# Spectral filter plus token mixer: the array shapes of two TensorE steps in the filter stage

## The chip, the cores and the metric

The kernel runs on one core of a Trainium2 chip. The metric is the device time of one execution in microseconds, and lower is better. Times of the kernel before are the median of three runs, and one execution was taken with the hardware profiler.

## The reference

The input is a matrix of 2048 tokens by 640 channels. Two kinds of layer alternate, and each pair is applied twice:

```python
# A: spectral filter
X = rfft2(layernorm(x), axes=(tokens, channels))   # 2048 x 321 complex
x = x + irfft2(X * (w_r + 1j * w_i))
# B: token mixer
h = layernorm(layernorm(x))
u = gelu(einsum("bsd,sf->bdf", h, w1) + b1)        # over the 2048 tokens, F = 1728
x = x + (einsum("bdf,fs->bds", u, w2) + b2).T
# x = A, B, A, B with the same weights
```

All of it is in float32; the kernel splits operands into a high and a low float16 part and multiplies three products (high by high, high by low, low by high).

## The kernel before

A filter layer is written as matrix products. The transform over the tokens is done in two factors, 2048 = 128 x 16, and the transform over the channels in one. Step by step, with the names of the code:

- `a0` normalizes and folds the rows and multiplies by the first token factor (table `tM`). Its output is `s1h` and `s1l`, the high and the low half of one array.
- `a1` is the **filter stage**. It is the part that is changed, and it runs twice in the program (from 60 to 130 us and from 560 to 628 us of the profiled span). It works through 16 groups, g = 0 to 15, and one group takes these steps:
  - **d** (`dstage`): the transform over the channels. The stationary operand is a piece of `s1h` or `s1l` (or `stk`, a stack of remainders that a DMA puts together), and the table `tD` streams through. The output is a PSUM tile `ps` with two banks, `ps[:, 0]` and `ps[:, 1]`.
  - **ph**, **pl** (`psplit`): ScalarE copies `ps` to float16 (`ph`), VectorE takes the rest (`pl`).
  - **s**: the second token factor (table `tS2`, seen as `tS` in the profile). In groups 3 to 12 it is done in two halves, **sA** and **sB** (`s2half`), each as three rounds of four 64x64 tiles of the array; in the other groups as full 128x128 products.
  - **ta**, **tb** (`term`, VectorE): the product with the filter. **sa**, **sb** (GpSimd): real and imaginary parts are put together in `ta`.
  - **xh** (ScalarE), **xl** (GpSimd): the high and the low half. **uh**, **ul** (ScalarE): a copy of 63 columns to the end of `xh` and of `xl` (in the profile `xh<-xh` and `xl<-xl`).
  - **i** (`is2mm`): the inverse of the second token factor, for three blocks of 128 columns. `xh` or `xl` is the stationary operand, and the table `tI2` (`tI` in the profile) streams through, 128 columns at a time.
  - **Yh**, **Yl**: the result is split again, by ScalarE and VectorE.
- `a2` does the inverse transforms over the channels and the tokens (table `tDi`, then `tIM`) and adds the result to x. Then comes the mixer (`b1st` and `b2nd`), in which TensorE multiplies almost without a pause.

The order of all instructions in the filter stage is written out by hand (`self.pin` keeps it). `group(g)` gives it for groups 3 to 12: d of the next group, sA, ph of the next group, uh, ta and tb of the group before, i of three groups back, sB, sa and sb, xl, Yl, pl, Yh, xh. So TensorE's order in such a group is d, sA, i, sB. Groups 13 to 15 follow a list of their own, `LAST`.

PSUM has four buffers of two banks (`big()`), which go round: d, s and i of a group take one each. So the tile of i is the one that s of two groups before it had written; it comes free when ta and tb have read it. `tb(g-1)` stands right before `i(g-3)` in the order.

`follow` adds waits for the two halves of s: `uh` waits for sA, and sB waits for that `uh`. In group 4, GpSimd issues two table DMAs (`tDi`, `tIM`) between sb and xl.

`HALF = [slice(0, 64), slice(64, 128)]`. The shape of a matmul in the array follows from its operands: rows from the partitions that it contracts, columns from the partitions of the output that it writes. The profile gives it as rows*columns (128*64).

Of the kernel before, what the change touches and what calls it, by code (L numbers as in the profile page):

```python
# [22 lines left out]
NX = 5  # L23
# [43 lines left out]
class Layers:  # L67
# [365 lines left out]
    def a1(self, first):  # L433
# [11 lines left out]
        xs = []  # L445
# [48 lines left out]
        HALF = [slice(0, 64), slice(64, 128)]  # L494

        def prods(a, b):

            return [(a[0], b[0]), (a[0], b[1]), (a[1], b[0])]

        def dstage(g):  # L500
            ps = self.big()
            part = lambda t: tuple(s[:, t * 16 + g].rearrange("p h a b -> p (h a b)") for s in (self.s1h, self.s1l))
            for c, bk, o0, o1, k in CL:
                table = lambda i: (self.tD[:, i, :o1 - o0], self.tD[:, i + 1, :o1 - o0])
                terms = prods(part(c), table(2 * c))
                if g < G0:
                    terms += prods(part(4), table(8 + 2 * c))
                else:
                    terms.append((stk[g - g % NC][:k, c, g % NC], self.tD[:k, 16 + c, :o1 - o0]))
                for i, (a, b) in enumerate(terms):  # L510
                    for o, f in zip(HALF, HALF[::-1]) if bk else [(slice(0, 128),) * 2]:
                        mm(ps[o, bk, o0:o1], a[:, f], b, start=i == 0, stop=i == len(terms) - 1)
            return ps

# [51 lines left out]
        def is2mm(ps, g, lt):  # L566

            sp = 1 if g == 0 else 0
            out = slice(128 * lt, 128 * lt + 128)

            for ri in range(2):
                for k, (a, b) in enumerate(((0, 0), (0, 1), (1, 0))):
                    for q in range(2):
                        r = slice(64 * q, 64 * q + 64)
                        mm(
                            ps[:, q, out], xs[g % NX][a][r, ri, out], self.tI2[r, b, sp, ri],
                            start=ri == 0 and k == 0, stop=ri == 1 and k == 2,
                        )

# [35 lines left out]
        w = {g: wload(g) for g in range(3)}  # L615
        pp, ps2, pv = {}, {}, {}
        ps = dstage(0)
        pp[0] = tuple(self.t(p, [128, 2, 322], F16, a, 2) for a in ("ph", "pl"))
        sc = PQS / (S1S * TS)
        for q in range(2):  # L620
            a, b, c = ps[:, q, :NL], pp[0][0][:, q, :NL], pp[0][1][:, q, :NL]
# [7 lines left out]
        def do(op):  # L629
            name, g, c, dve = re.fullmatch(r"([a-zABY]+)(\d+)([ab]?)(!?)", op).groups()  # L630
            g, W = int(g), V if dve else G
            pair = lambda: (tt[g][0], tt[g][1])
            if name == "d":
                dst[g] = dstage(g)
            elif name == "ph":
                dst[g] = psplit(dst[g])
# [15 lines left out]
            elif name == "sa":  # L652
                suma(pair(), part[c], W)
            elif name == "sb":
                ins = sumb(pair(), part[c], W)
                if g == 3:
                    with self.after(ins):
                        nc.gpsimd.dma_start(self.tDi, A["tDi"])
                        nc.gpsimd.dma_start(self.tIM0, A["tIM"][:, 0:4])
            elif name == "xh":  # L660
                xhi(g, part[c], tt[g][0][:, :, part[c]])
            elif name == "xl":
                xlo(g, part[c], tt[g][0][:, :, part[c]], W)
            elif name in ("uh", "ul"):
                ins = twice(g, name == "ul")
                if name == "uh" and g > 1 and g + 2 in half:
                    follow(ins, half[g + 2])
                    half[g + 2] = ins
            elif name == "sA":
                ps2[g] = self.big()  # L670
                half[g] = s2half(ps2[g], pp[g], 0)[1]
            elif name == "sB":
                follow(s2half(ps2[g], pp.pop(g), 1)[0], half.pop(g))
            elif name == "i":
                pv[g, c] = self.big()
                for lt in range(3)[ltile[c]]:
                    is2mm(pv[g, c], g, lt)
            elif name == "Yh":
                yhi(g, pv[g, c], ltile[c])
            elif name == "Yl":  # L680
                ylo(g, pv[g, c], ltile[c])
# [67 lines left out]
        g = NG - 3  # L749
# [1300 lines left out]
```

## Time and profile before

| | |
|---|---|
| median of three runs | 1007.59 us (1006.79 to 1008.24) |
| profiled execution, its own time | 1004.95 us |
| span of the profiled execution, first to last instruction | 1002.9 us |
| TensorE busy (PE) | 962.0 us, 96% |
| weight loads busy (PEld) | 709.7 us, 71% |
| VectorE (DVE), ScalarE (ACT), GpSimd (POOL) | 782.2, 575.7, 297.1 us |
| mean granted TensorE clock | 0.978 |

How to read it: PE is the matmul part of TensorE and PEld its weight loads, which run beside the matmuls. Matmuls are pipelined, so the duration of one is longer than its share of the time; what counts is the distance from the start of one to the start of the next. All engine instructions carry line 59, that of a helper, so rows are told apart by the names of their tiles. In a timeline a row may merge several instructions (x4), and its first number is the start of the first one.

### The profile page before, as it was taken

The numbers are of one execution on the slowest core, as the hardware profiler recorded it, in microseconds if no ns is written. First come the engines' busy times: TensorE is split into PE (matmuls) and PEld (weight loads), VectorE is DVE, ScalarE is ACT, GpSimd is POOL, SyncE is SP. The second block draws the span as 40 slices with busy tenths as digits, with TensorE's granted clock in tenths as the row PEclk, the third lists the DMA queues.
The fourth block names the chain that finished last, engine by engine and source line by source line (L and its number), as shares of the span: only waits on it lengthen the run. The fifth ranks groups of instructions, "written<-read, shape, count | busy, mean of one in ns | idle before, by whom it ended". The sixth has DMA issues, their size and how long they took to land.

```text
span 1002.9 us, 22044 instructions
## 1 busy us (share of the span) xinstructions
PE 962.0 (96%) x8747; PEld 709.7 (71%) x8747; DVE 782.2 (78%) x1493; ACT 575.7 (57%) x888; POOL 297.1 (30%) x500
## 2 busy tenths in 40 slices
PE   4899999999999999999999799999999999999998
PEld 3776777677777777777777677776777777677776
DVE  7979989989677784666677699789956567998885
ACT  5857759698666465555544377585643444444531
POOL 6928757422122102222223287573000000000000
PEclk9589999999999999999999899999999999999999
DMA  7865357757667546464331554474544447655411
GB/s 233 277 183 179 95 192 234 246 202 272 222 216 262 193 149 210 127 210 130 127 104 74 167 181 128 147 229 169 183 156 166 146 131 252 232 170 199 145 46 53
DMA packets 67263, 176.51 MB, mean 176 GB/s; under 512 B 7996, under 2 KB 15320, under 8 KB 67160
## 3 DMA queue, kind: packets, MB, share of 16 engines
q1 hardware_dynamic: 59384, 146.92, 45.4%
q0 software_dynamic: 7776, 28.20, 7.6%
q8 instruction: 68, 1.11, 0.5%
q14 instruction: 35, 0.29, 0.1%
HBM read 127.24 MB, written 47.84 MB: 175 GB/s over the span
## 4 chain that ended last, share of the span: by engine, by line
PE 53%; DVE 23%; ACT 7%; POOL 6%; issue 5%; DMA 4%; SPq 1%; ACTq 0%; DVEq 0%; POOLq 0%
PE ps L59 53%; DVE wl L59 3%; DVE st L59 3%; DMA xt<-x 3%; DVE f L59 3%; POOL eo L59 3%; DVE xt L59 2%; DVE s1l L59 2%; ACT z L59 1%; POOL xt L59 1%; ACT wh L59 1%; DVE hl L59 1%; DVE Yl L59 1%; DVE ta L59 1%; ACT junk L59 1%
## 5 line engine op out<-in xcount | busy, mean ns | idle before, releaser
L59 PEld LDWEIGHTS <-wh 128*128 128x128 f16 x2602 | 251.5, 98 | 100.8 <-issue 2.4
L59 PEld LDWEIGHTS <-wl 128*128 128x128 f16 x1610 | 157.5, 98 | 62.2 <-issue 1.0
L59 PE MATMUL ps<-ul,wh 128*128 128x320 f16 x448 | 133.1, 299 | 0.0
L59 PE MATMUL ps<-uh,wl 128*128 128x320 f16 x448 | 133.1, 299 | 0.0
L59 PE MATMUL ps<-uh,wh 128*128 128x320 f16 x416 | 124.3, 299 | 0.0
L59 PE MATMUL ps<-hl,wh 128*128 128x320 f16 x496 | 102.2, 299 | 0.8 <-DVE hl L59 0.8
L59 PEld LDWEIGHTS <-wo 128*128 128x128 f16 x756 | 73.9, 98 | 29.4 <-DVE wo L59 0.8
L59 DVE SCALAR_TENSOR_TENSOR wl<-raw,s,wh 128x896 f16<-128x896 f32 (+2 forms) x62 | 74.0, 1198 | 20.5 <-ACT wh L59 17.7
L59 POOL TENSOR_TENSOR r<-v,mh 128x1 f32<-128x1 f32 x64 | 37.0, 578 | 158.2 <-DVE nm L59 149.0
L59 ACT ACTIVATE junk<-raw 128x896 bf16<-128x896 f32 (+1 forms) x60 | 59.6, 993 | 27.8 <-DMA raw<-w 24.5
L59 PE MATMUL ps<-tDi,Yh 128*128 128x322 f16 x320 | 71.3, 300 | 0.2
L59 ACT ACTIVATE wh<-raw,s 128x896 f16<-128x896 f32 (+2 forms) x66 | 66.6, 1033 | 4.4 <-DMA w1A<-wh 3.9
L59 DVE TENSOR_TENSOR f<-eo 128x256 f32<-128x256 f32 (+1 forms) x124 | 39.1, 368 | 37.0 <-POOL eo L59 36.2
L59 POOL TENSOR_TENSOR xt<-xt,ec 128x320 f32<-128x320 f32 x64 | 52.9, 848 | 31.6 <-DVE xt L59 31.6
L59 ACT ACTIVATE z<-xt,nb,r 128x640 f32<-128x640 f32 x31 | 28.5, 920 | 54.1 <-POOL z L59 43.1
L59 PE MATMUL ps<-u,wo 128*128 128x320 f16 x420 | 59.0, 299 | 0.5 <-DVE wo L59 0.5
L59 DVE BATCH_NORM_STATS2 st<-xt 128x6 f32<-128x320 f32 x126 | 55.3, 481 | 4.9 <-DMA xt<-x 4.4
L59 PE MATMUL ps<-hha,wh 128*128 128x320 f16 x288 | 58.1, 299 | 0.9 <-DVE wh L59 0.9
L59 PE MATMUL ps<-tM,f 128*128 128x128 f32 x160 | 40.6, 437 | 18.7 <-DVE f L59 18.7
L59 POOL TENSOR_TENSOR eo<-z 128x320 f32<-128x320 f32 x60 | 52.3, 893 | 17.2 <-ACT z L59 15.2
L59 PE MATMUL ps<-tDi,Yl 128*128 128x322 f16 x192 | 55.7, 299 | 1.7 <-DVE Yl L59 1.7
L59 PE MATMUL ps<-hha,wl 128*128 128x320 f16 x256 | 53.4, 299 | 0.0
(252 smaller groups left out, 2351.5 us busy)
## 6 DMA issues: line engine op xcount, KB each, us to landing
xt<-x SPq DMA_DIRECT2D x79, 320.0 KB
raw<-w SPq DMA_DIRECT2D x32, 512.0 KB
w<-w SPq DMA_DIRECT2D x48, 321.0 KB
x<-xt SPq DMA_DIRECT2D x47, 320.0 KB
raw<-w SPq DMA_DIRECT2D x32, 448.0 KB
raw<-w2z SPq DMA_DIRECT2D x32, 448.0 KB
w1S<-sp POOLq DMA_DIRECT2D x20, 512.0 KB, 3.7
out<-xt SPq DMA_DIRECT2D x15, 320.0 KB
```

Of the source, the lines that this page charges most:

```text
L59: i = f(*a, **k)
```

## The change

Two places in the filter stage. In d, the first bank was written by matmuls of the full 128x128 array and the second bank by pairs of matmuls in two 128x64 column tiles (with the halves crossed over); now both banks are written by pairs in 128x64 tiles, the first with the halves in order. In i, each product was a pair of matmuls in two 64x128 row tiles; now it is four matmuls in four 64x64 tiles, like those of sA and sB. Nothing else is touched: the tables, the products, the PSUM banks and the order of the steps stay.

```diff
@@ dstage
                 for i, (a, b) in enumerate(terms):
-                    for o, f in zip(HALF, HALF[::-1]) if bk else [(slice(0, 128),) * 2]:
+                    for o, f in zip(HALF, HALF[::-1] if bk else HALF):
                         mm(ps[o, bk, o0:o1], a[:, f], b, start=i == 0, stop=i == len(terms) - 1)
@@ is2mm
             for ri in range(2):
                 for k, (a, b) in enumerate(((0, 0), (0, 1), (1, 0))):
-                    for q in range(2):
-                        r = slice(64 * q, 64 * q + 64)
+                    for q, c in ((0, 0), (0, 1), (1, 1), (1, 0)):
+                        x = xs[g % NX][a][HALF[q], ri, out]
                         mm(
-                            ps[:, q, out], xs[g % NX][a][r, ri, out], self.tI2[r, b, sp, ri],
+                            ps[HALF[c], q, out], x[:, HALF[c]], self.tI2[HALF[q], b, sp, ri],
                             start=ri == 0 and k == 0, stop=ri == 1 and k == 2,
                         )
```

In groups 3 to 12 the array's shape went 128x128, 128x64 (d), 64x64 (sA), 64x128 (i), 64x64 (sB), and so changed five times from one group to the next. Now it goes 128x64 (d), 64x64 (sA, i, sB) and changes twice.

## The prediction

> **What bounds the kernel now.** I read the page first, then the groups by form, the timeline of one group of the filter stage, the waits, and last the chain of waits at both ends of the stage.
>
> ```profile
> span 1002.9 us, 22044 instructions
> ...
> PE 962.0 (96%) x8747; PEld 709.7 (71%) x8747; DVE 782.2 (78%) x1493; ACT 575.7 (57%) x888; POOL 297.1 (30%) x500
> ```
> ```profile
> L59 PE MATMUL ps<-tI,xh 64*128 64x128 f16 x768 | 36.4, 217 | 2.5 <-DVE tb L59 2.4
> L59 PE MATMUL ps<-tI,xl 64*128 64x128 f16 x384 | 33.9, 216 | 2.0 <-POOL xl L59 1.3 <-ACT xl L59 0.5
> ```
>
> TensorE looks like the bound of everything, at 96%. But a busy PE only says that some pipelined matmul is under way. The second view counts step i: 1152 matmuls are 36 in each of 32 steps (16 groups, two stages). The timeline of one group of the second stage decides more than the 96%:
>
> ```profile
> 595.71 0.31 PE L59 MATMUL ps<-tD,s1h 128*128 128x160 f16 x2
> ...
> 596.15 0.23 PE L59 MATMUL ps<-tD,s1l 128*128 128x161 f16 x1
> 596.22 0.23 PE L59 MATMUL ps<-tD,stk 98*128 98x161 f16 x1
> 596.38 0.33 PE L59 MATMUL ps<-tD,s1h 128*64 128x160 f16 x4
> ...
> 596.70 0.88 DVE L59 SCALAR_TENSOR_TENSOR tb<-ps,sx,w 128x642 f32<-128x642 f32 x1
> ...
> 596.90 0.24 PE L59 MATMUL ps<-tD,stk 96*64 96x161 f16 x2
> ...
> 597.07 0.33 PE L59 MATMUL ps<-ph,tS 64*64 64x321 f16 x4
> 597.23 0.31 PE L59 MATMUL ps<-pl,tS 64*64 64x321 f16 x4
> ...
> 597.37 0.31 PE L59 MATMUL ps<-ph,tS 64*64 64x321 f16 x4
> ...
> 597.63 0.29 PE L59 MATMUL ps<-tI,xh 64*128 64x128 f16 x4
> ...
> 598.42 0.82 DVE L59 SCALAR_TENSOR_TENSOR pl<-ps,ph 128x642 f16<-128x642 f32 x1
> ...
> 598.59 0.22 PE L59 MATMUL ps<-tI,xl 64*128 64x128 f16 x2
> 598.74 0.33 PE L59 MATMUL ps<-ph,tS 64*64 64x321 f16 x4
> ...
> 599.04 0.31 PE L59 MATMUL ps<-ph,tS 64*64 64x321 f16 x4
> ...
> 599.27 0.32 PE L59 MATMUL ps<-tD,s1h 128*128 128x160 f16 x2
> ...
> 599.46 0.89 DVE L59 SCALAR_TENSOR_TENSOR ta<-ps,sx,w 128x642 f32<-128x642 f32 x1 [0.22 <-POOL ta L59]
> ...
> 600.27 0.88 DVE L59 SCALAR_TENSOR_TENSOR tb<-ps,sx,w 128x642 f32<-128x642 f32 x1
> ...
> 601.20 0.29 PE L59 MATMUL ps<-tI,xh 64*128 64x128 f16 x4
> ```
>
> A group takes 599.27 - 595.71 = 3.56 us. Start to start, a matmul of 161 columns takes 0.07 (596.15 to 596.22), a round of four 64x64 tiles with 321 columns 0.14 (597.23 to 597.37), and the 18 pairs of i 0.0565 each (17 steps from 597.63 to 598.59). What is more than this pace at a change of shape is the change's cost: full to 128x64 0.16 - 0.07 = 0.09; 128x64 to 64x64 0.17 - 0.07 = 0.10; 64x64 to 64x128 0.26 - 0.14 = 0.12; 64x128 to 64x64 0.15 - 0.06 = 0.09; 64x64 to full 0.23 - 0.14 = 0.09. The first round of 64x64 after a change is 0.16 instead of 0.14, so 0.02 more. It is the shape that costs, not the new tile: from s to d, both in the full array, no time is lost (68.56 to 68.69, the usual 0.13).
>
> ```profile
> 68.56 0.30 PE L59 MATMUL ps<-ph,tS 128*128 128x321 f16 x1
> 68.69 0.30 PE L59 MATMUL ps<-tD,s1h 128*128 128x160 f16 x2
> ```
>
> So PE has work or changes of shape for the whole 3.56 us. Yet it is not alone in this. tb, started at 600.27, ends at 601.15, and i begins at 601.20, 0.05 later; one group before, tb ends at 597.58 and i begins at 597.63, again 0.05 later. i takes the PSUM tile that tb has just read. The waits of seven groups of each stage (584.0 to 613.0 us, then 86.0 to 113.0 us) say the same, for the weight loads that open step i:
>
> ```profile
> PEld L59 <- DVE tb L59: 1.9, 7, 0.3
> ```
> ```profile
> PEld L59 <- DVE tb L59: 4.6, 7, 1.3
> ```
>
> Seven waits in seven groups. There is a loop: last round of sB to ta 0.42 (599.04 to 599.46; the row blames GpSimd, but sB's last round ends later, at 599.35), ta to tb 0.81, tb to i 0.93, i to sB 1.11 (597.63 to 598.74), sB first to last round 0.30. The sum is 3.57, the whole period. The loop and PE's own work are equally long by accident. A saving counts in full only where it lies on both.
>
> **The change part by part.** *Step d, first bank.* 8 full matmuls a group (12 in the first two groups) become as many pairs. The second bank's pairs already run like this: from 596.38 the seven pairs before 596.90 take 0.52, 0.074 each with the 0.02 of entry, so a pair costs what a full matmul does. The change inside d goes, 0.09 a group. It lies between sB and sA, outside the loop: PE reaches sA earlier and then waits longer for tb. Worth nothing in groups 3 to 12, as long as the loop holds.
>
> *Step i, shape.* sA to i changes no shape now: 0.12 less, but i begins when tb is done, so nothing for the time. i to sB changes no shape: 0.09 less, inside the loop. sB's first round then needs no entry, 0.02 less; i, which begins after a wait, pays some 0.01 more for its first loads. Together 0.10 off the loop: 3.47 a group. PE's own work falls to 3.56 - 0.09 - 0.12 - 0.09 - 0.02 = 3.24, and DVE, which waits 0.22 before ta, keeps 0.12 of that. Neither becomes the bound.
>
> *Step i, instructions.* 36 matmuls and 36 loads become 72 and 72. Four 64x64 tiles in sB do in 0.14 what a full array does, so four at 128 columns should keep a pair's pace, 0.0565 for a round. What the trace does not show is whether 8 instructions can be supplied in 0.0565 us, 7 ns each, 144 times on end. Bounds: i now needs 4 in 0.0565, 14 ns each, and that pace is set by the columns, so the supply is at least this fast. And behind a change of shape they come much faster:
>
> ```profile
> 597.06:597.12 0.06, 0.06 (x8) 0.05 (x8) 0.06 (x1) 0.06 (x1) 0.00 (x0) 1.00 0.19 51
> ```
>
> Eight loads and the four matmuls of sA's first round begin in these 0.06 us (the other four PE records are older), 5 ns each. So at least 12 stand ready behind a change. I take 0.0565 for a round, nearest to this row, and keep 8 x 14 = 0.113 as the other end. Weight loads that precede a round are off the path: in sB they begin with the round before.
>
> *Start of the stages.* There the order is d, d, s, s, and nothing waits for tb:
>
> ```profile
> 61.59 0.23 PE L59 MATMUL ps<-tD,s1l 128*128 128x161 f16 x1
> 61.76 0.33 PE L59 MATMUL ps<-tD,s1h 128*64 128x160 f16 x4
> ...
> 62.56 0.23 PE L59 MATMUL ps<-tD,s1l 128*64 128x161 f16 x2
> 62.72 0.32 PE L59 MATMUL ps<-tD,s1h 128*128 128x160 f16 x2
> ...
> 63.51 0.23 PE L59 MATMUL ps<-tD,s1l 128*128 128x161 f16 x1
> 63.67 0.33 PE L59 MATMUL ps<-tD,s1h 128*64 128x160 f16 x4
> ```
>
> Three changes, each 0.16 or 0.17 with the matmul's 0.07, so 0.09 to 0.10; with the dearer entries about 0.11 each, 0.33 a stage, on PE's path to the first ta. Later d's beside a full s only shift a change from the middle of d to its front: nothing.
>
> *Groups 3 to 5, second stage.* i of group 3 has no wait and sheds both of its changes. sB follows `uh` or `ph`, so ScalarE must keep up:
>
> ```profile
> 575.82 0.71 ACT L59 ACTIVATE ph<-ps 128x642 f16<-128x642 f32 x1 [1.97 <-PE ps L59]
> ...
> 577.52 0.89 DVE L59 SCALAR_TENSOR_TENSOR ta<-ps,sx,w 128x642 f32<-128x642 f32 x1
> ...
> 579.28 0.75 POOL L59 TENSOR_TENSOR ta<-ta,tb 128x321 f32<-128x321 f32 x1 [0.20 <-DVE tb L59]
> ...
> 584.12 0.30 ACT L59 ACTIVATE xh<-xh 128x126 f16<-128x126 f16 x1
> ...
> 584.47 0.33 PE L59 MATMUL ps<-ph,tS 64*64 64x321 f16 x4
> ```
>
> ph, which sB of group 3 follows, ends at 576.53; sB could start about 0.2 earlier than before and still after it. ta moves by that 0.2, and GpSimd's sa, its two table DMAs, xl, then `uh` (584.12 + 0.30) and sB (584.47) with it. Worth 0.2. In the first stage VectorE and GpSimd are in a row there, so I take 0 (0 to 0.2).
>
> *Loop.* From sB of group 5 to tb of group 11 there are six passes of i to sB: 6 x 0.10 = 0.60 a stage. Behind that the list of the last groups takes over:
>
> ```profile
> 114.08 0.31 ACT L59 ACTIVATE xl<-xl 128x126 f16<-128x126 f16 x1 [0.29 <-POOL xl L59]
> ...
> 115.01 0.83 DVE L59 SCALAR_TENSOR_TENSOR pl<-ps,ph 128x642 f16<-128x642 f32 x1 [0.38 <-ACT ph L59]
> ```
>
> pl waits for ph, ph stands behind ul (114.08), and ul waits for GpSimd's xl, which goes back to tb of group 11. So the last pass and the change saved before d of group 14, 0.2 together, are not taken (0 to 0.2).
>
> *Sum.* First stage 0.33 + 0.60 = 0.93, second 0.33 + 0.2 + 0.60 = 1.13, together 2.1 us. Behind each stage come products that PE does without a pause, so nothing gives this back. The profiled execution took 1004.95 us (span 1002.9), 2.64 under the median of 1007.59; 2.1 less is 1002.85 for it, and 1005.5 against the median. With 0.2 more at three places it is 1004.8, and with the six passes alone (1.2) 1006.4.
>
> **The rivals.**
>
> *The supply of instructions becomes the bound of i (slower).* If instructions come 14 ns apart and only a few stand ready, a round takes 0.113 and i 18 x 0.113 = 2.03 instead of 1.02. It decides from 0.062 a round (7.8 ns an instruction) on, where 0.10 a group is used up. The loop then has 0.92 more a group, 6 x 0.92 = 5.5 a stage; the first groups add about 2, and the four steps i at the end of the list about 3, where DVE's queue hides the rest. Some 10 a stage, 20 in all, less the 0.7 of the starts: 1027. With a longer lead it is less; the middle is about 1018. For it: no row shows more than 12 instructions at 7 ns or less. Against it: those 12, and that PE has 0.2 us in each wait for tb to get ahead. [...]
>
> [...]
>
> *PE alone is the bound (faster by far).* If tb's 0.05 were chance and i could start earlier, all three changes would count: 0.32 in each of 20 groups and 0.7 at the starts, 7 us, 1000.5. Against it are 14 waits in 14 groups.
>
> [...]
>
> **How the numbers follow.** About 0.2% (2.0 us) is what a measurement of this kernel can tell from no change. The forecast, 1005.5, has 0.56; it lies on that line, so I give 0.30 to faster and 0.26 to same. Slow supply has 0.28, slow supply with a lead (and shapes that cost nothing) 0.10, of which 0.08 same and 0.02 slower; PE alone 0.06. Faster 0.30 + 0.06 = 0.36, same 0.26 + 0.08 = 0.34, slower 0.28 + 0.02 = 0.30. The forecast's own range is 1004.8 to 1006.4. The range to hold 8 in 10 leaves out PE alone (0.06) and the upper half of slow supply (0.14): 1004.0 to 1018.0.
>
> **What would show it.** Right: i's 18 rounds still 0.0565 apart; i to sB 0.06 instead of 0.15; no gap inside d or from sA to i beyond the wait; groups of 3.47 us; i still 0.05 behind tb, with PE idle 0.2 before it. Wrong: rounds of i further apart than 0.062, or a period of 3.56 although the changes are gone, or one under 3.4, which would mean that tb wasn't what i waits for.

## The result and the profile after

The change makes the kernel slower: 1016.58 us median (1012.41 to 1016.98, four runs) against 1007.19 (1004.22 to 1008.24, four runs), ratio 1.0093, 95% interval 1.0072 to 1.0115. The profiled execution after took 1016.96 us, 12.0 more than the one before. I had forecast 1005.5, within 1004.0 to 1018.0. The time lies in the range, in the part that belonged to the slow-supply rival, and not at the forecast. That it comes so near that rival's middle value, 1018, is chance: what costs the time is another mechanism, as the section on the prediction says.

The page of the kernel after, span, busy times and the instruction queue:

```profile
span 1014.9 us, 24892 instructions
...
PE 961.9 (95%) x10171; PEld 713.8 (70%) x10171; DVE 783.2 (77%) x1493; ACT 575.8 (57%) x888; POOL 296.6 (29%) x500
...
q8 instruction: 79, 1.29, 0.5%
```

and the same queue on the page of before:

```profile
q8 instruction: 68, 1.11, 0.5%
```

PE is as busy as before (962), and 12 us more of the span are idle. The third row becomes the important one: queue q8, the one that the page calls instruction, moves 1.29 MB in 79 packets, 16 KB each.

The windows by stage, from the first product of d to the first with `tDi` (length, then busy time and count of each engine), before and then after:

```profile
60.09:129.16 69.07, 64.20 (x1327) 48.25 (x1327) 60.43 (x106) 47.63 (x99) 46.36 (x56) 1.00 0.48 143
559.83:626.64 66.81, 64.74 (x1320) 49.31 (x1321) 56.15 (x85) 41.23 (x84) 45.75 (x55) 0.97 0.52 160
```
```profile
60.45:135.26 74.81, 64.18 (x2038) 50.74 (x2039) 61.06 (x108) 47.76 (x99) 46.36 (x56) 0.98 0.46 140
564.37:639.23 74.86, 64.93 (x2032) 51.70 (x2033) 57.67 (x88) 41.25 (x84) 45.66 (x55) 0.96 0.48 144
```

The first filter stage is 5.7 us longer and the second 8.0; all other parts together are 1.8 shorter. PE's work in the stages is the same, but its instructions have gone from 2654 to 4077 in the first. Next TensorE's waits after, from 60 to 140 and from 562 to 645 us (total, times, longest). Before, these windows have no row of the kind:

```profile
PE ps L59 <- issue: 5.3, 5, 2.1
```
```profile
PE ps L59 <- issue: 8.3, 8, 2.0
```

"issue" is idle time for which the profile has no other engine and no transfer to name. The timeline of the second stage shows where it stands (PE after, from 591 us, then the group from 598.70):

```profile
591.52 0.31 PE L59 MATMUL ps<-tI,xh 64*64 64x128 f16 x8
591.66 0.23 PE L59 MATMUL ps<-tI,xl 64*64 64x128 f16 x4
591.71 0.28 PE L59 MATMUL ps<-tI,xh 64*64 64x128 f16 x8
593.72 0.25 PE L59 MATMUL ps<-tI,xl 64*64 64x128 f16 x4 [1.72 <-issue]
```
```profile
598.70 0.33 PE L59 MATMUL ps<-tD,s1h 128*64 128x160 f16 x4
...
599.68 0.88 DVE L59 SCALAR_TENSOR_TENSOR tb<-ps,sx,w 128x642 f32<-128x642 f32 x1
...
600.61 0.31 PE L59 MATMUL ps<-tI,xh 64*64 64x128 f16 x8
...
600.80 0.28 PE L59 MATMUL ps<-tI,xh 64*64 64x128 f16 x7
...
601.70 0.21 PE L59 MATMUL ps<-tI,xh 64*64 64x128 f16 x1 [0.62 <-issue]
...
601.95 0.30 PE L59 MATMUL ps<-tI,xh 64*64 64x128 f16 x8
...
602.12 0.30 PE L59 MATMUL ps<-tI,xh 64*64 64x128 f16 x8
...
602.40 0.24 PE L59 MATMUL ps<-tI,xl 64*64 64x128 f16 x4
...
602.45 0.32 PE L59 MATMUL ps<-ph,tS 64*64 64x321 f16 x4
```

i begins 0.05 behind tb (599.68 + 0.88 = 600.56), its rounds run at the forecast pace (601.95 to 602.12 for three, 0.057 each), and sB follows 0.05 behind i's last round. Then TensorE stops once, in i's fifth round, for nothing that is on the list of waits. Numbering TensorE's instructions in their order of start shows a rule (matmuls, loads and the 79 semaphore waits and drains of the program together). Between 590 and 615 us the distances of over 0.25 us from start to start inside i, other than before its first round, lie in front of instructions 12226, 12482, 12738, 12994, 13250 and 13506, so 256 apart. A q8 packet seems to hold as many: the kernel after has 20,421 TensorE instructions and 79 packets, the one before 17,573 and 68, both times 258 a packet. The windows from stop to stop count it (127 or 128 matmuls and as many loads each, since a row's matmul can begin a few ns outside the window):

```profile
593.71:597.42 3.71, 3.60 (x127) 2.72 (x127) 2.26 (x4) 2.54 (x5) 1.16 (x2) 1.00 0.32 108
597.42:601.69 4.27, 3.62 (x128) 2.73 (x128) 3.90 (x7) 2.57 (x5) 3.40 (x5) 1.00 0.38 101
601.69:605.67 3.98, 3.62 (x127) 2.73 (x127) 3.05 (x5) 2.55 (x5) 2.53 (x3) 1.00 0.43 117
```

A group before has 168 TensorE instructions. After it has 168 + 16 (d) + 72 (i) = 256, exactly one block.

### The profile page after: what moved, and what is told of

Its sections match the earlier page's. It is cut to its first block, busy times and chain, and to the rows that moved or that the text cites. A ratio compares the mean times of both kernels' runs of the same rounds, so it can differ in the third digit from the quotient of the medians.

```text
span 1014.9 us, 24892 instructions
## 1 busy us (share of the span) xinstructions
PE 961.9 (95%) x10171; PEld 713.8 (70%) x10171; DVE 783.2 (77%) x1493; ACT 575.8 (57%) x888; POOL 296.6 (29%) x500
## 3 DMA queue, kind: packets, MB, share of 16 engines
q8 instruction: 79, 1.29, 0.5%
## 4 chain that ended last, share of the span: by engine, by line
PE 42%; DVE 23%; issue 13%; ACT 10%; POOL 8%; DMA 4%; SPq 0%; POOLq 0%; ACTq 0%; DVEq 0%
PE ps L59 42%; DVE wl L59 4%; DVE f L59 3%; DVE st L59 3%; POOL eo L59 3%; DVE s1l L59 2%; DVE xt L59 2%; DMA xt<-x 2%; ACT wh L59 1%; ACT z L59 1%; ACT junk L59 1%; POOL xt L59 1%; DVE hl L59 1%; ACT xt L59 1%; POOL w1A L960 1%
```

## The experiments

Theory A: the program reaches TensorE in blocks of 256 instructions, and a dense stretch runs out of them. A border is the place between two blocks; *standing* is the time in which TensorE does nothing at a border. Rival B: a round of four 64x64 tiles with 128 columns is slow by itself. Rival C: the column tiles in d cost. In its first form A said that a stop depends on where a block's border lies in the group (how much dense work stands ahead of it); in its second form, from the ninth run on, that a block simply can't come sooner than some 3.4 to 3.7 us after the one before.

**One part alone.** d in pairs of 128x64 tiles, i as before:

```diff
-                    for o, f in zip(HALF, HALF[::-1]) if bk else [(slice(0, 128),) * 2]:
+                    for o, f in zip(HALF, HALF[::-1] if bk else HALF):
```

> Only step d is changed (both banks in 128x64 pairs), step i stays in two 64x128 tiles. TensorE has 184 instructions in a group of 3 to 12 instead of 168 before and 256 after. Theory A (TensorE's instructions come in blocks of 256, and a block is usable some 2.4 us after its fetch begins; where TensorE gets through its instructions faster than that, it stands at the block's border): hardly more instructions, so no gap inside i at a border, and only the starts of the two stages gain, 0.7 us: 1006.5 us, ratio 0.999. Theory B (64x64 rounds of 128 columns are slow in themselves): the same. Theory C (column tiles in d are what costs): slower by most of the 9.4 us, 1014 us or more.

1006.28 us, ratio 1.0009 (0.9998 to 1.0019). C has fallen. Nor is there a gain, not even the expected 0.7 us of the starts (0.999 lies outside the interval). In the loop, i of two groups starts at 598.03 and 601.60, still 3.57 apart, though the shape no longer changes inside d. That is the forecast's "worth nothing as long as the loop holds". The profiled execution has one stop of 0.9 us. It stands behind the two table loads of group 4: the border before it is passed at 583.36, the next fetch begins only at 587.21, as these loads run out, and its block is in use at 589.62.

i in four 64x64 tiles, d as before (the second half of the diff), 240 instructions a group:

> Only step i is changed (four 64x64 tiles), step d stays half full, half 128x64. 240 TensorE instructions a group. Theory A: a gap every 256 instructions, which moves by 16 from group to group, so that some fall in i and some elsewhere; slower by 4 to 10 us: 1011 to 1017 us. Theory B: slower by about the whole 9.4 us, with rounds of i evenly further apart than 0.0565 us. Theory C: no slower than before, 1006.5 us.

1013.62 us, ratio 1.0074 (1.0047 to 1.0101). So i brings the loss. But the starts of i in this run's timeline, in groups without a stop inside i, are what the prediction's loop said:

```profile
600.50 0.31 PE L59 MATMUL ps<-tI,xh 64*64 64x128 f16 x8
...
603.96 0.31 PE L59 MATMUL ps<-tI,xh 64*64 64x128 f16 x8
...
607.43 0.31 PE L59 MATMUL ps<-tI,xh 64*64 64x128 f16 x8
```

3.46 and 3.47 a group, against 3.57 before.

**More instructions, no change of shape.** The kernel before, with each pair of i split into two halves of 64 columns; the same work and shapes, and 240 instructions a group:

```diff
-                        for q in range(2):
+            for h in (0, 64):          # outermost; ri and k inside
+                        for q in range(2):
...
-                            ps[:, q, out], ..., self.tI2[r, b, sp, ri],
+                            ps[:, q, out.start + h:out.start + h + 64], ..., self.tI2[r, b, sp, ri, h:h + 64],
```

> The kernel before with both shapes as they were, but each matmul of step i with 128 columns is split into two of 64 columns: 72 matmuls and 72 weight loads in i as after, 240 TensorE instructions a group, in two 64x128 tiles; a pair of 64 columns needs 0.029 us of the array, so the array's work is almost the same. Theory A: gaps at the borders of blocks as in the changed kernel, slower by 4 to 10 us: 1011 to 1017 us. Theory B or C (the shapes are slow): 1007 to 1009 us, no gaps.

1018.21 us, ratio 1.0123 (1.0090 to 1.0156), above A's range of 1011 to 1017. No tile is 64x64 here in i, and the loss is no smaller: B has fallen. In this run, too, TensorE stops with "issue" (3.9 and 2.9 us in the two windows). The instructions at which it stops leave 194 when their numbers are divided by 256, as 12226 and its followers do in the kernel after (12226 = 47 x 256 + 194). So does every "issue" stop in these two windows of all the kernels here and below, 91 in all, at the border or at most two instructions behind it.

**Where the border lies.** Dummy matmuls of one column at the very start, where TensorE waits for its data in any case (the first product of the kernel after starts at 11.68 us), move all borders. With 100, 62, 76 and 20 of them (62 shown):

```diff
+        self.pin = True
+        for _ in range(2):
+            ps = self.big()
+            for _ in range(31):
+                self.PE.matmul(ps[:, 0, :1], self.ones, self.ones[:, :1], start=True, stop=True)
+        self.pin = False
```

> The changed kernel with 100 one-column matmuls at the very start, where TensorE has nothing to do: 200 instructions that shift every border of 256 by 200. A group of the changed kernel has just 256 instructions (64 in d, 24 in sA, 144 in i, 24 in sB), so the border falls at the same place of every group, now about 40 instructions into i; with the shift it falls some 100 instructions into i. Theory A: the instructions before the border are then all of i, which are used up in 0.7 to 1.0 us instead of 1.9, and the gap grows from about 0.5 to 1.4 us a group, all of it in the loop: about 1026 us (1020 to 1032), with the gaps at the 12th round of i instead of the 5th. Theory B: where the border falls changes nothing, 1016.6 us (1012 to 1018).

> The change, with 62 one-column matmuls (124 TensorE instructions) before the first transform, where TensorE waits for its data anyway. They move every border between two blocks of 256 instructions: counted from the first instruction of i, from about 136..126 to 12..2 in the first filter stage's groups and from about 39..33 to 171..165 in the second's, that is out of i (instructions 0 to 143) but for its first dozen. Theory A (each block of 256 arrives some 2.35 us after its fetch starts, and TensorE stands at a border when it has used up the about 100 instructions ahead of it in less): 1006 us, range 1003.5 to 1010, as only the last groups of each stage still have a border inside dense i. A rival that charges a border the same wherever it lies, or the count of instructions alone: 1016.6, as after.

> The change, with 76 one-column matmuls (152 instructions) at the start: the borders go to about 240 of 256 in the first stage's groups (in s, between d and the next i) and to about 143 in the second's, the very end of i, where the 97 instructions ahead are all of i and last 0.7 us. Theory A: first stage as fast as before, second some 1.2 to 1.65 us a group slower, so 1018, range 1013 to 1024, all of it after 575 us. The rival (a border costs the same wherever it lies): 1016.6, in both stages.

> The change, with 20 one-column matmuls (40 instructions) at the start: borders at about 96..86 of i in the first stage, at 255..249 (the end of s, before i) in the second. Theory A: the second stage runs free (i starts 3.46 us apart), the first loses 0.3 to 1.0 us a group, so 1011, range 1007 to 1015, all of the loss before 135 us. The rival (the same cost wherever a border lies): 1016.6, in both stages.

Measured: 1018.01 (ratio 1.0125, 1.0084 to 1.0165), 1018.14 (1.0108, 1.0091 to 1.0126), 1015.27 (1.0093, 1.0067 to 1.0119) and 1019.32 us (1.0128, 1.0107 to 1.0149). All four are about as slow as after. The stops moved with the borders (the numbers stay, the groups move), but they did not go away. With 62 matmuls they stand at the start of d in the second stage, where the first form of A expected none:

```profile
593.72 0.26 PE L59 MATMUL ps<-tD,s1h 128*64 128x160 f16 x2 [1.42 <-issue]
...
598.46 0.30 PE L59 MATMUL ps<-tD,s1h 128*64 128x160 f16 x3 [1.35 <-issue]
...
602.46 0.30 PE L59 MATMUL ps<-tD,s1h 128*64 128x160 f16 x3 [0.56 <-issue]
```

So the position rule was wrong. Its 1006 for this run missed by 12 us, its 1026 with 100 dummies by 8 and its 1011 with 20 by 8. With 76 its time fits, but 6.0 of the 12.1 us of standing lie in the first stage, where it expected none. "A border costs the same wherever it lies" came nearer. The control, the kernel before with the same 62 dummies:

> The kernel before, with the same 62 one-column matmuls at the start. Its group has 168 instructions, so its borders fall elsewhere in each group whatever the shift. Theory A: within 0.15% of the kernel before, ratio 0.9985 to 1.0015; that also tells what the added matmuls cost by themselves (nothing). Were it faster or slower by more, the padding itself would move the time, and the other runs had to be read with that.

1006.63 us, ratio 1.0005 (0.9992 to 1.0018), and no "issue" row: the dummies themselves cost nothing.

**Fewer instructions on the average.** Four 64x64 tiles in i of the odd groups up to 11, the rest as before: in dense groups 240 instructions, on the average 204.

```diff
+            if g % 2 and g < 12:
+                ... # the four 64x64 tiles
+                return
```

> The kernel before with four 64x64 tiles in i for the odd groups up to 11 only (group of 240 TensorE instructions), the even ones and the last three as before (168). Theory A in its second form (a block of 256 instructions takes at least some 3.4 to 3.7 us from border to border, so what counts is how many instructions a period of 3.5 us uses): 204 a group on the average, 4.4 us a block, so next to no standing at borders (under 1.5 us in all, against 17.5 after), and the 0.1 us of the odd groups is left: ratio 0.9985 to 1.0010. A rival by which a dense stretch of i (144 instructions in 1.04 us) is enough to make a border cost, whatever the group uses: half of the 12.2 us of standing that i alone had, ratio 1.003 to 1.006.

1006.93 us, ratio 1.0007 (0.9996 to 1.0018). The one "issue" row of this run in the two windows:

```profile
PE ps L59 <- issue: 0.4, 1, 0.4
```

The stops are gone although half of the groups have the same dense i. A dense i alone is not enough; the mean use of instructions fits, and that is A's second form. (The 17.5 and 12.2 us of standing in this expectation and the next are counted from start to start at the borders; the "issue" rows, which count from the end of the last matmul, give 13.6 and 9.2 for the same runs, and the text goes by these.)

**Who is in the way of a fetch.** After, with the filter's weights loaded once a stage (321 KB a group less; all groups are multiplied by group 0's weights):

```diff
         def wload(g):
+            if g > 0:
+                return w0[0]
             ...                            # the load; w0 keeps the first tile
```

> The change with the filter's weights loaded once a stage instead of for every group (321 KB a group less; all groups use group 0's weights). It tells why fetches start late. If instruction fetches are held up by the kernel's other transfers, the fetch comes sooner after the border, the standing at borders falls from 17.5 us to under 9 and the time to 1004 to 1010. If the fetch has its own pace, the standing stays between 12 and 20 us and the time between 1012 and 1019.

1012.23 us, ratio 1.0055 (1.0040 to 1.0071). The standing meets the first expectation and the time the second. The two "issue" rows fall from 5.3 and 8.3 to

```profile
PE ps L59 <- issue: 2.4, 3, 1.4
```
```profile
PE ps L59 <- issue: 4.7, 4, 2.2
```

So in the profiled executions about half of the standing goes with the weights' loads. That of this run was the fastest of its four (1009.14 us). By the ratios the loss falls from 0.93 to 0.55%, by two fifths. The kernel before was not run without these loads, so what they cost it is not known. The transfers of the kernel after from 594 to 596 us, in slices of 0.05 us, show how:

```profile
GB/s 411 308 514 267 503 267 524 257 411 205 257 226 287 328 236 205 174 164 113 103 72 72 62 62 369 21 0 0 0 0 0 0 0 0 0 0 0 0 0 0
```

The loads run out, and in the slice at 595.20 stands a spike of 369: 16 KB in 0.05 us are 328, so this is the fetch. The block is in use at 597.42, 2.2 us later (each border has one packet ahead of it, which I take for its block). All six fetches between 590 and 613 us begin so, where a load thins out. It is not always that of `w`: its packets are of 2,568 bytes, those of the stacked remainders (`stk`) of 512. Here the last packet of `w` begins before 594.7, and what runs out at 595.2 is the load of `stk` behind it. In three of the six it is `w`, in three `stk`, which the run without the weights' loads still has.

**The supply by itself.** 600 matmuls of i's kind at the start of the kernel before (beside its first loads), and then 800 behind its last product, where nearly nothing else is transferred and nothing waits for anything:

```diff
+        ...                            # H: the two halves; the order is kept by self.pin
+        for _ in range(4):             # 3 at the start
+            ps = self.big()
+            for _ in range(50):
+                for q, c in ((0, 0), (0, 1), (1, 1), (1, 0)):
+                    self.PE.matmul(ps[H[c], q, :128], self.ones[H[q], H[c]], self.ones[H[q]], start=True, stop=True)
```

> The kernel before, with 600 matmuls of i's kind (64x64, 128 columns, four tiles in turn, on a tile of ones) at the start, where nothing waits for them and they wait for nothing: 1200 instructions, at most 5 borders. Theory A: 0.056 us a round of four inside a block (256 instructions in 1.8 us), and TensorE stands at the borders so that these come 3.4 us or more apart: the 150 rounds take 13 to 17 us instead of the 8.4 that they hold. A rival (the borders cost only because instructions wait for other engines in between): 8.4 to 10 us, with no standing above 0.2 us. The kernel's time rises by what of it does not fit into the 11 us in which TensorE waits for its data: 3 to 6 us by A.

> The kernel before, with 800 matmuls of i's kind (64x64, 128 columns, four tiles in turn, on a tile of ones) behind its last product, where nearly no other transfer runs and nothing waits: 1600 instructions, six or seven borders. At the start (the run before this in the study) such a block took 3.7 to 5.6 us from border to border, with the fetch 1.1 to 2.8 us behind the border. If the fetch's pace is its own, the blocks here take that too, 3.4 us or more. If the kernel's transfers are what makes fetches late, they take less: at the least the 1.8 us that 256 instructions last by themselves, and then there is no standing. I expect 3.2 to 3.6 us a block, a fetch about 1.05 us behind the border and usable 2.3 us later, so 20 to 25 us more than the kernel before.

One execution each, so mainly the traces count (1013.37 us, 7.5 over the median before, where 3 to 6 was expected; 1028.04 us, 20.7 over one execution before, as expected). At the start the 150 rounds take 18.0 us, more than the expected 13 to 17:

```profile
1.12 5.27 PE L59 MATMUL ps<-ones 64*64 64x128 bf16 x223 [1.12 <-DVE ones L122]
9.54 3.63 PE L59 MATMUL ps<-ones 64*64 64x128 bf16 x128 [3.16 <-issue]
13.54 2.88 PE L59 MATMUL ps<-ones 64*64 64x128 bf16 x128 [0.38 <-issue]
17.27 1.89 PE L59 MATMUL ps<-ones 64*64 64x128 bf16 x121 [0.84 <-issue]
```

and at the end:

```profile
1005.73 1.98 PE L59 MATMUL ps<-ones 64*64 64x128 bf16 x128 [0.30 <-issue]
1009.20 1.98 PE L59 MATMUL ps<-ones 64*64 64x128 bf16 x128 [1.49 <-issue]
1012.95 1.98 PE L59 MATMUL ps<-ones 64*64 64x128 bf16 x128 [1.76 <-issue]
1016.69 1.98 PE L59 MATMUL ps<-ones 64*64 64x128 bf16 x128 [1.76 <-issue]
1020.71 2.85 PE L59 MATMUL ps<-ones 64*64 64x128 bf16 x128 [2.04 <-issue]
```

This is the disputed cost alone. 128 matmuls and 128 loads are done in 1.98 us (a round of four starts every 0.056), and then TensorE stands for 1.5 to 2.0 us until the next block is there. The blocks start 3.47, 3.75, 3.74 and 4.02 us apart. The transfers between 1009 and 1013 us (0.1 us a slice) hold one packet:

```profile
GB/s 0 0 0 0 0 0 0 0 0 0 0 0 0 164 0 0 0 0 0 0 0 0 0 0 0 0 0 0 0 0 0 0 0 0 0 0 0 0 0 0
```

It begins at 1010.3, 1.1 us behind the border at 1009.20, and its block is in use at 1012.95, 2.6 us later. So even where nearly nothing else is transferred a block costs 1.1 + 2.6 = 3.7 us here, or 14.6 ns an instruction, and no fetch begins here before the block of the one before it is in use (those behind the borders at 1009.20 and 1012.95 begin at 1010.3 and 1014.05). My 3.2 to 3.6 us was somewhat too low. 3.7 is no hard limit: the closest two fetches in the trace after begin 3.42 us apart (626.32 and 629.74).

## Why the prediction was wrong, point by point

Everything in one table. The period is that of the second stage, from the start of i of group 4 to that of group 12 over 8; a block is period x 256 / instructions; both stages is the length of the two filter stages together, from the first product of d to the first with `tDi`; standing is the sum of the two stages' "issue" rows. These four are of the profiled execution, the ratio is of all runs.

| kernel | instructions a group | period, us | block, us | both stages, us | standing, us | ratio |
|---|---|---|---|---|---|---|
| before | 168 | 3.62 | 5.52 | 135.9 | 0 | 1 |
| before + 62 dummies | 168 | 3.64 | 5.55 | 136.0 | 0 | 1.0005 |
| d alone | 184 | 3.75 | 5.22 | 136.8 | 0.9 | 1.0009 |
| odd groups | 204 (mean) | 3.66 | 4.59 | 138.4 | 0.4 | 1.0007 |
| i alone | 240 | 3.70 | 3.95 | 143.8 | 9.2 | 1.0074 |
| i split, old shape | 240 | 3.74 | 3.99 | 144.8 | 6.8 | 1.0123 |
| after, `w` once | 256 | 3.92 | 3.92 | 142.3 | 7.1 | 1.0055 |
| after | 256 | 4.25 | 4.25 | 149.7 | 13.6 | 1.0093 |
| after + 62 dummies | 256 | 4.38 | 4.38 | 149.8 | 16.4 | 1.0108 |
| after + 100 | 256 | 4.25 | 4.25 | 145.7 | 9.6 | 1.0125 |
| after + 76 | 256 | 4.12 | 4.12 | 149.6 | 12.1 | 1.0093 |
| after + 20 | 256 | 4.48 | 4.48 | 149.6 | 12.0 | 1.0128 |

No kernel averages a block in under 3.9 us, and those that would need one sooner stand. The loop asks for 256 instructions in 3.46 us. They come in 3.47 to 4.02 where nearly nothing else is transferred and in 4.25 on the average beside the loads of the stage; that is the loss of the middle groups. In the last groups, where steps i follow each other closely, single stops reach 2.0 us. Of the 2.5 us by which the two stages of the odd-groups run are longer than before, 1.4 lie ahead of the first i, where nothing is changed.

*"Step i, instructions" is the step that failed.* I asked whether 8 instructions can come in 0.0565 us, took 0.0565 from the 12 that came in 0.06, and kept 14 ns an instruction as the other end. Both ends are true, at different lengths. Inside a block the instructions come at 7 ns each (8 a round of 0.056 us); over blocks at 14 to 16 ns where nearly nothing else is transferred, and at 17 in the second stage after. A row that shows 12 instructions bounds a burst, not 256 of them, and not the mean of a group. The right sum was the one that I didn't make: instructions of a group against what the supply gives in a period. A trace of before could have given it a bound: between 618 and 623 us its transfers hold

```profile
q8 instruction: 2, 0.03, 2.7%
```

two fetches, 3.8 us apart, the closest that I later found in the stages of before. Nothing there showed 256 instructions in less than 3.8 us, and the change needed them in 3.46. By 3.8 the loss is 0.23 a group instead of a gain of 0.10. (3.8 was what that place asked for; before never asked for more, so its trace alone could not show the limit.)

*The slow-supply rival* had the direction and nearly the price of an instruction (14 ns), but its mechanism was another: it spread the price over each round of i and came to 1027. Rounds keep 0.056; what is lost comes once in 256 instructions, and nothing is lost where a group leaves the time for it (no standing before, at 5.52 us a block). No run shows the lead that this rival and the slow supply with a lead put into their sums, beyond the 12 instructions of the row of before: in the runs, what stands ready is what is left of a block of 256, up to 32 rounds on end in the run with 800 matmuls behind the last product. The packets are of 16 KB, the stops lie 256 instructions apart, and with 14 ns a matmul they last up to 2.1 us in the kernel after.

*Loop and shapes were right in the second stage.* Where no stop falls, the period is 3.46 (forecast 3.47), i is 0.05 behind tb, i to sB costs 0.05. The change in d alone brings nothing in the loop. In the first stage the forecast took the same six gains of 0.10, and that was too much. There the starts of i before are 3.57, 4.63, 4.32, 4.32 and 3.57 apart in the last five passes; in the kernel after with 62 dummies, which has no stop in them, 3.46, 4.53, 4.32, 4.33 and 3.46. Two of these steps, before and then with 62 dummies:

```profile
103.24 0.28 PE L59 MATMUL ps<-tI,xh 64*128 64x128 f16 x4 [0.70 <-DVE tb L59]
...
107.56 0.28 PE L59 MATMUL ps<-tI,xh 64*128 64x128 f16 x4 [0.71 <-DVE tb L59]
```
```profile
101.86 0.31 PE L59 MATMUL ps<-tI,xh 64*64 64x128 f16 x8 [1.01 <-DVE tb L59]
...
106.18 0.31 PE L59 MATMUL ps<-tI,xh 64*64 64x128 f16 x8 [0.91 <-DVE tb L59]
```

In the two groups of 4.32 VectorE does a piece of the mixer's weights (`wl`) between ta and tb, and nothing is gained; what they hang on instead was not tested. So the five passes gain 0.32 instead of 0.50.

*Start of the stages, groups 3 to 5.* From the first d to the first i it was 15.12 us before and is 14.67 after in the first stage (0.45 less, forecast 0.33), in the second 15.87 and 15.30 (0.57 less, forecast 0.33). All kernels with the new d have the same TensorE work in this stretch. They take 14.67 to 16.27 us in the first stage and 15.12 to 16.06 in the second, those with the old d 14.99 to 16.56 and 15.41 to 16.12. The medians differ by 0.33 and 0.52, as forecast or more, but the spread is larger than the gain, so it is likely and not shown. The 0.2 of group 3 lies behind the start of its i: from there to the next i it is 3.65 before and 3.52 after, 0.13 of the 0.2, and then a stop falls.

*PE alone as the bound* and *shapes that cost nothing* are out: the first by the 3.57 of d alone, the second by the 3.46 of i alone.

What stays open: what starts a fetch. With nearly nothing else transferred it begins 1.1 us behind the border (at 1009.20 and at 1012.95); beside the kernel's loads, in all six cases between 590 and 613 us, where a load thins out, which the smaller standing without the weights' loads supports but doesn't prove. That the split i loses more time than i alone with less standing (6.8 against 9.2) lies mostly outside of the filter stages: of the 4.4 us between the two profiled executions the stages have 1.0, to which its longer period where it doesn't stop (3.62) adds 0.05 a group. The other parts have 3.4, and they take 864 to 870 us in the twelve kernels of the table (867 before) though nothing in them was changed but for the dummies. So a few tenths of a per cent between two rows say little. None of the versions was faster than the kernel before: what the shapes give back (0.10 a group) would need, as an estimate from the row of the odd groups, about 200 instructions a group or fewer with i in 64x64 tiles, and such a kernel I didn't find.

## What to carry to other kernels

Before matmuls are split into smaller tiles, count the TensorE instructions (a matmul is two, with its load: 10,171 of each in the kernel after) of one period of the loop, not only the pace of a round: here 256 instructions took 3.5 to 4.0 us where nearly nothing else was transferred and some 4.2 beside the stage's loads, so that at 240 or more in 3.5 us TensorE stood and at 204 on the average hardly. The sign in these profiles was "issue" idle in the middle of a step, 256 instructions apart, with a packet of the instruction queue 2.2 to 2.9 us ahead of its end. A bound must be read from a row as long as what it is to bound: twelve instructions say nothing about 256.

## What the hardware showed unexpectedly

- TensorE's instructions came in packets of 16 KB, 256 at a time by the distance of the stops (20,421 instructions and 79 packets in the kernel after), and at its stops a block was in use 2.2 to 2.9 us after its packet began, though the packet itself took 0.9 to 1.4 us.
- With nearly nothing else transferred, blocks started 3.47 to 4.02 us apart, while their 256 instructions ran in 1.98 us.
- Between 590 and 613 us of the kernel after, beside its loads, fetches began 1.3 to 3.0 us behind the border ahead of them (elsewhere in its filter stages from 0.3 before to 3.9 behind it), against 1.1 at two borders with nearly nothing else transferred. Without 321 KB of weights a group, the standing of the profiled execution went from 13.6 to 7.1 us.
- Within a block four 64x64 tiles did take 128 columns every 0.056 us, 14 ns a matmul, for 32 rounds on end (128 matmuls in 1.98 us).
